# fp32 value products on two column halves of TensorE

## The chip, the cores and the metric

The kernel runs on one core of one Trainium2 chip. The metric is the device time of one execution in microseconds (us), the median over runs. Lower is better.

## The reference, cut to what matters

The program computes a causal sliding-window attention with a linear distance bias, and feeds its output to a mixture of eight experts in which every token goes to one expert.

```python
# B=8 batches, H=8 heads, S=576 positions, D=64, window 128
scores = scale * np.matmul(q, k.transpose(0, 1, 3, 2))
mask = (rel >= 0) & (rel < window)
scores = np.where(mask, scores + bias[None], -1e9)
attn = np.exp(scores - np.max(scores, axis=-1, keepdims=True))
attn = attn / (np.sum(attn, axis=-1, keepdims=True) + 1e-09)
attn_out = np.matmul(attn, v)                       # the value products
x = attn_out.transpose(0, 2, 1, 3).reshape(4608, 512)
expert_idx = np.argmax(normalized(x) @ normalized(expert_emb).T / tau, axis=1)
out[mask_e] = gate_w[mask_e, None] * (np.maximum(x[mask_e] @ w1[e], 0) @ w2[e])
```

## The kernel before

**Tiles.** The 4608 tokens are cut into 36 tiles of 128 queries: per two batches, a "first" tile and three "full" tiles of each batch, and one "pair" tile that holds the last 64 queries of both. So there are 8 first, 24 full and 4 pair tiles. Every tile is worked on in two half steps of four heads (`hf`), which makes 72 half steps.

**A half step.** `score_pe` makes the scores (a bias product on line 600 or 591, then q by k on line 613) in PSUM; it already works in 64-row and 64-column parts of the array. VectorE merges the two parts of the window (`merge_dve`) and takes the row maximum (`max_dve`, line 630). ScalarE takes the exponential (line 637). TensorE transposes the probabilities (`probs_pe`, line 645, output `ptp`), ScalarE copies them to SBUF as `pq` (line 655). GpSimd masks them into `md`, the part that meets the tile's own keys, and `mp`, the part that meets the keys of the tile before (line 664; for a pair tile `md` is the buffer `tails`, line 673). A first tile has one part alone and uses `pq` itself.

**The values.** `values_pe` (lines 685 to 706) then multiplies by the values. For each head the masked probabilities (128 keys by 128 queries, fp32) are the stationary operand and the values (128 keys by 65 columns; the last column is a constant and gives the row sum) are the moving operand. The result, queries on the partitions, goes to one PSUM bank `av`. A product of two bf16 constants (`erow`, `eone`, line 692) opens the accumulation of the sums' column. A full tile makes two products of 128 columns for each head; a pair tile makes one product of 128 columns and two of 64 columns, because its two halves have different earlier tiles; a first tile makes one. After that VectorE takes reciprocals (line 722) and normalizes (line 728), and the token rows are split in fp16 parts, transposed by a DMA (`xT`, line 759), routed, and scattered to DRAM (`xs`, line 870).

**The order.** All of attention is one static plan: class `Plan` schedules jobs with written costs (in ns), due times and buffer counts, and emits each engine's instructions in the order that comes out. The cost of the value products is on line 1085; `SWITCH` is 60 and `STEP`, the planned distance of two half steps, 2600. Every engine then runs its list in order. Near the end of attention the plan also fetches and splits the weights of the commonest expert (lines 915 to 922) and runs its first products (`ps_head`, lines 950 and 974) as filling work. After the last tile come the last routing steps, the scatters, and the experts (lines 1463 to 1652), a second plan.

Of the kernel before, what the change touches and what calls it, by code (L numbers as in the profile page):

```python
# [23 lines left out]
P = 128  # L24
# [54 lines left out]
SWITCH = 60  # L79
# [5 lines left out]
def share(T, f):  # L85
    return int((T + 1) * f + 1e-6) > int(T * f + 1e-6)
# [122 lines left out]
def kernel(  # L209
# [11 lines left out]
    nc = tc.nc  # L221
    B, _, H2, S = kx.shape
    H, D = 2 * H2, P // 2
    NTOK, DM = out.shape
    E, _, F = moe_w1.shape
# [3 lines left out]
    REM = S - NF * P  # L229
# [33 lines left out]
    def bank(what, shape, name):  # L263
        return banks["pool"].tile(shape, F32, tag=RING[what], name=name, bufs=BANKS[RING[what]])
# [17 lines left out]
    erow = const.tile([P, P], BF16, name="erow")  # L282
    eone = const.tile([P, 4], BF16, name="eone")
    nc.vector.memset(eone, 1.0)
    nc.gpsimd.memset(erow, 0.0)
    for n in (2, 1, 0):
        nc.gpsimd.affine_select(
            erow, erow, pattern=[[0, P]], compare_op=ALU.is_gt, fill=eparts[n], base=-n, channel_multiplier=1
# [170 lines left out]
    def attention(actx):  # L459
# [10 lines left out]
        qT, kT, vS = {}, {}, {}  # L470
# [81 lines left out]
        def k_blocks(T):  # L552
            kind, b, t = tiles[T]
            return [b, b + 1] if kind == "pair" else [b]
# [17 lines left out]
        def prevs(T):  # L572
            kind, b, t = tiles[T]
            if kind == "first":
                return None
            if kind == "full":
                return T - 1
            return (T - 1 - NF, T - 1)
# [39 lines left out]
        def merge_dve(T, hf, j):  # L618
            kind, b, t = tiles[T]
            ps = sc[T, hf, j]  # L620
            if kind == "full":
                m = mk["full"].unsqueeze(1).to_broadcast([P, 2, P])
                nc.vector.copy_predicated(ps[:, :, 0:P], m, ps[:, :, P : 2 * P])  # L623
            elif kind == "pair":
                m = mk["pair"][:, 0:REM].unsqueeze(1).to_broadcast([P, 2, REM])
                nc.vector.copy_predicated(ps[:, :, 0:REM], m, ps[:, :, P : P + REM])

        def max_dve(T, hf, j):
            nm_t[T, hf, j] = sm.tile([P, 2], F32, tag="nm", name=f"nm{j}_{T}_{hf}", bufs=8)
            nc.vector.tensor_reduce(nm_t[T, hf, j], sc[T, hf, j][:, :, 0:P], axis=AX.X, op=ALU.min)  # L630
# [10 lines left out]
        def probs_pe(T, hf):  # L641
            pe = pr_t.pop((T, hf))
            pt = bank("ptp", [P, 4, P], name=f"ptp_{T}_{hf}")
            for i in range(4):
                nc.tensor.transpose(pt[:, i, :], pe[:, i, :], ident)  # L645
            pq_t[T, hf] = pt
# [38 lines left out]
        def values_pe(T, hf):  # L685
            kind, b, t = tiles[T]
            md, mp = msk.pop((T, hf))
            px = bank("av", [P, 512], name=f"av_{T}_{hf}")[:, 0 : 4 * (D + 1)]
            px = px.rearrange("p (h d) -> p h d", h=4)
            xps[T, hf] = px  # L690
            pv_ = prevs(T)
            nc.tensor.matmul(px[:, :, D], erow, eone, start=True, stop=False, skip_group_check=True)
            jobs = []
            for i in range(4):
                h = 4 * hf + i
                jobs.append((0, i, 0, 0, px[:, i], md[:, i], vS[T][:, h]))
                if kind == "pair":
                    for a in range(2):
                        o = slice(a * REM, (a + 1) * REM)
                        jobs.append((1, i, 1, a, px[o, i], mp[:, i, o], vS[pv_[a]][:, h]))  # L700
                elif pv_ is not None:
                    jobs.append((0, i, 1, 0, px[:, i], mp[:, i], vS[pv_][:, h]))
            jobs.sort(key=lambda z: z[:4])
            last = max(z[2] for z in jobs)
            for _, _, n, _, o_, a_, b_ in jobs:
                nc.tensor.matmul(o_, a_, b_, start=False, stop=(n == last), skip_group_check=True)  # L706

        groups = GROUPS
# [286 lines left out]
        def then(what, u, tail=""):  # L995
            return [(f"{what}{u}{tail}", ORDER)] if u >= 0 else []

        def due(stage, u):
            return STEP * u + 1000 * DUE[stage]
# [15 lines left out]
        last = None  # L1015
        for i, (e, ns, f) in enumerate(expert_ops()):
            last, prev = f"expert{i}", last
            key = ("expert", 0)
            J(
                last, e, ns, f, after=[prev] if prev else [], due=100 * i, early=EXPERT,  # L1020
# [4 lines left out]
        for T in range(NT):  # L1025
            kind, b, t = tiles[T]
            u0 = 2 * T
            pair = kind == "pair"
# [15 lines left out]
            for hf in range(2):  # L1044
                u = u0 + hf
                a = (T, hf)
                first = kind == "first"
                dep = [f"hi_q{T}"] + k_loads + (["tab_pair"] if pair else []) + ([] if first else ["factors"])
                J(
                    f"score{u}", "PE", (960 if first else 980 if pair else 970) + SWITCH, lambda a=a: score_pe(*a),  # L1050
                    makes=[(RING["sc"], ("sc", u, j)) for j in range(2)], after=dep + then("flip", u - 2),
                    uses=[("ldq", T)] + [("k", x) for x in k_blocks(T)],
                    due=due("score", u),
                )
                for j in range(2):
                    c, key, n = a + (j,), ("sc", u, j), f"{u}_{j}"
                    J(
                        f"merge{n}", "DVE", 0 if first else 215 if pair else 328, lambda c=c: merge_dve(*c),
                        after=[f"score{u}"], uses=[key], due=due("merge", u) + 670 * j,
                    )  # L1060
                    J(
                        f"max{n}", "DVE", 330, lambda c=c: max_dve(*c), after=[f"merge{n}"], makes=[("nm", ("nm", n))],
                        uses=[key, ("nm", n)], due=due("max", u) + 670 * j,
                    )
                    J(
                        f"exp{n}", "ACT", 502, lambda c=c: exp_act(*c),
                        after=[f"max{n}"] + ([(f"exp{u}_0", ORDER)] if j else []),
                        makes=[] if j else [("pe", ("pe", u))], uses=[key, ("nm", n), ("pe", u)],
                        due=due("exp", u) + 670 * j,
                    )  # L1070
                J(
                    f"flip{u}", "PE", 452 + SWITCH // 2, lambda a=a: probs_pe(*a), after=[f"exp{u}_0", (f"exp{u}_1", -230)],
                    makes=[(RING["ptp"], ("ptp", u))], uses=[("pe", u)], due=due("flip", u),
                )
                J(
                    f"phi{u}", "DVE" if share(u, SHARE["p" if T < LATE else "p2"]) else "ACT", 592, lambda a=a: probs_act(*a), after=[f"flip{u}"], makes=[("pq", ("pq", u))],
                    uses=[("ptp", u)], due=due("phi", u),
                )
                J(
                    f"mask{u}", "POOL", 0 if first else 1260 if pair else 1188, lock=() if first else (480, 420, 600) if pair else (590, 590), emit=lambda a=a: mask_pool(*a), after=[f"phi{u}"] + (["tails"] if pair else []),  # L1080
                    makes=[] if first else [(f"tails{hf}" if pair else "md", ("md", u)), ("mp", ("mp", u))], uses=[("pq", u)], due=due("mask", u),
                )
                mk_ = [("pq", u)] if first else [("md", u), ("mp", u)]
                J(
                    f"av{u}", "PE", (480 if first else 1100 if pair else 920) + SWITCH // 2, lambda a=a: values_pe(*a),
                    after=[f"mask{u}", ] + then("put", T - XBUFS) + [f"load_v{x}" for x in k_tiles(T)], makes=[(RING["av"], ("av", u))],
                    uses=mk_ + [("v", y) for y in k_tiles(T)], due=due("av", u),
                )
                J(
                    f"recip{u}", "DVE", 95, lambda a=a: sums_dve(*a), after=[f"av{u}"], makes=[("rs", ("rs", u))],  # L1090
                    uses=[("av", u)], due=due("norm", u),
                )
                J(
                    f"norm{u}", "DVE", 332, lambda a=a: normalize(*a), after=[f"recip{u}"],
                    makes=[("xf", ("xf", T))] if hf == 0 else [], uses=[("av", u), ("rs", u), ("xf", T)],
                    due=due("norm", u) + 300,
                )
            u = u0 + 1
# [38 lines left out]
        for gi, G in enumerate(groups):  # L1137
            T0 = sum(groups[:gi])
            u = 2 * (T0 + G) - 1
# [3 lines left out]
            key = ("rank", gi)  # L1143
# [41 lines left out]
        u = 2 * GT - 1  # L1185
# [885 lines left out]
```

## Time and profile before

| what | value |
|---|---|
| median of 3 runs | 629.81 us (629.66 to 630.69) |
| the profiled execution's own time | 628.76 us |
| its span, first to last instruction | 627.0 us |
| granted TensorE clock, mean | 0.999 of full speed |
| TensorE (PE) busy | 608.8 us, 97% |
| weight loads (PEld) busy | 432.3 us, 69% |
| VectorE (DVE) busy | 464.0 us, 74% |
| ScalarE (ACT) busy | 355.6 us, 57% |
| GpSimd (POOL) busy | 256.8 us, 41% |

The busy time of an engine is the time in which at least one of its instructions was under way. Matmuls overlap one another, so the duration of one matmul is longer than its distance to the next, and a busy PE is not one at its peak; the distance of starts tells what a stream of matmuls costs. An fp32 product appears in the trace as two matmul instructions, each with a weight load of its own. In a shape such as 128*64 128x65, the first pair is the rows and columns of the stationary operand, the second the partitions and elements of the moving one.

### The profile page before, as it was taken

Reading aid. Unit: us, or ns where it says so; the run is one execution under the profiler, and the core shown is the slowest. Engines: PE = TensorE matmul, PEld = TensorE weight load, DVE = VectorE, ACT = ScalarE, POOL = GpSimd, SP = SyncE. Lnnn points to the kernel's source line nnn. Section 1 sums busy time; section 2 is a strip of 40 time slices with the busy share of each in tenths; the row PEclk is TensorE's granted clock in tenths of the full one; section 3 lists DMA queues with packets and bytes.
Section 4 is the critical chain, followed back from the end, with each engine's and each line's share of the span. In section 5 each row is a group of like instructions: output and inputs, shape, how many; then the busy total and the mean of one; then the engine's idle time right before and its main releaser. Section 6 shows DMA issues by size and latency. Waiting matters only on the chain.

```text
span 627.0 us, 15235 instructions
## 1 busy us (share of the span) xinstructions
PE 608.8 (97%) x5573; PEld 432.3 (69%) x5573; DVE 464.0 (74%) x1184; ACT 355.6 (57%) x822; POOL 256.8 (41%) x450
## 2 busy tenths in 40 slices
PE   6999999999999999999999999999999999999995
PEld 4788887888787788646465476475584764764885
DVE  4666577567758788742678778879999998789692
ACT  4777676767756787313445227447458375367441
POOL 7535457846855856750110501300403414103342
PEclk9999999999999999999999999999999999999999
DMA  8896787988997899549994945935929859516001
GB/s 215 186 157 136 194 181 182 233 183 172 231 197 163 253 229 220 135 154 304 184 295 79 338 121 106 331 89 134 323 64 290 229 91 331 125 46 174 31 2 68
DMA packets 163836, 112.48 MB, mean 179 GB/s; under 512 B 122533, under 2 KB 134821, under 8 KB 163760
## 3 DMA queue, kind: packets, MB, share of 16 engines
q1 hardware_dynamic: 153600, 85.24, 55.6%
q0 software_dynamic: 10160, 26.26, 15.3%
q8 instruction: 44, 0.72, 0.5%
q14 instruction: 32, 0.26, 0.2%
HBM read 72.93 MB, written 19.70 MB: 148 GB/s over the span
## 4 chain that ended last, share of the span: by engine, by line
PE 82%; DVE 6%; ACT 3%; DMA 3%; issue 2%; SPq 1%; POOL 1%; POOLq 0%; ACTq 0%; DVEq 0%
PE ps L1640 20%; PE av L706 18%; PE sc L613 7%; PE ptp L645 6%; PE ps7d L1483 5%; PE ps7c L1483 5%; PE ps7a L1483 5%; PE ps L1463 4%; PE sc L600 3%; PE ps7b L1483 3%; PE ps_t L1630 2%; PE ps_head L950 1%; ACT pe L637 1%; ACT w1h L1388 1%; DMA ldq<-q_dram 1%
## 5 line engine op out<-in xcount | busy, mean ns | idle before, releaser
L452 POOL DMA_INDIRECT out_dram<-y,ids x32 | 44.9, 1404 | 212.5 <-ACT y L1652 148.1
L637 ACT ACTIVATE pe<-sc,nm 128x128 f32<-128x128 f32 x288 | 85.3, 371 | 21.7 <-DVE nm L630 16.8
L1640 PE MATMUL ps<-w2h,hh 128*128 128x512 f16 x224 | 84.9, 379 | 1.3 <-ACT hh L1606 1.3
L1640 PE MATMUL ps<-w2h,hl 128*128 128x512 f16 x224 | 84.9, 379 | 0.4 <-DVE hl L1604 0.4
L1640 PE MATMUL ps<-w2l,hh 128*128 128x512 f16 x224 | 84.9, 379 | 0.0
L1640 PEld LDWEIGHTS <-hh 128*128 128x128 f16 x448 | 43.5, 98 | 53.3 <-ACT hh L1606 1.7
L706 PE MATMUL av<-v,mp 128*128 128x65 f32 (+1 forms) x512 | 79.8, 263 | 0.0
L1483 PEld LDWEIGHTS <-w1h 128*128 128x128 f16 x672 | 65.7, 98 | 14.8 <-issue 0.3
L706 PE MATMUL av<-v,md 128*128 128x65 f32 x384 | 75.6, 278 | 0.0
L655 ACT COPY pq<-ptp 128x512 f32<-128x512 f32 x72 | 42.1, 585 | 38.6 <-PE ptp L645 36.6
L706 PEld LDWEIGHTS av<-v,mp 128*128 128x128 f32 (+1 forms) x512 | 62.7, 178 | 0.7
L630 DVE TENSOR_REDUCE nm<-sc 128x2 f32<-128x256 f32 x144 | 56.1, 411 | 4.8 <-PE sc L613 4.6
L706 PEld LDWEIGHTS av<-v,md 128*128 128x128 f32 x384 | 58.5, 192 | 1.7 <-POOL ig L830 0.9
L613 PE MATMUL sc<-k,ldq 64*64 64x192 f32 (+1 forms) x1024 | 59.1, 325 | 0.0
L645 PE MATMUL ptp<-ident,pe 128*128 128x128 f32 x288 | 47.7, 285 | 3.5 <-ACT pe L637 3.0
L623 DVE COPY_PREDICATED sc<-mask_full,sc 128x256 f32<-128x256 int32 x96 | 37.6, 423 | 16.0 <-PE sc L613 14.4
L613 PEld LDWEIGHTS sc<-k,ldq 64*64 64x64 f32 (+1 forms) x1024 | 41.6, 143 | 9.8 <-issue 4.0
L755 POOL TENSOR_TENSOR gx<-xf,gx 128x512 f16<-128x512 f32 x36 | 42.1, 1169 | 13.5 <-DVE gx L744 11.5
L664 POOL TENSOR_SCALAR_AFFINE_SELECT md<-pq 128x512 f32<-128x512 f32 x48 | 31.7, 660 | 37.8 <-ACT pq L655 36.3
L722 DVE RECIPROCAL rs<-av 128x4 f32<-128x4 f32 x72 | 13.1, 181 | 46.0 <-PE av L706 45.8
L870 POOL DMA_INDIRECT xs<-gx,di x36 | 36.1, 1002 | 13.1 <-issue 5.0
L1652 ACT ACTIVATE y<-ps,gs 128x512 f32<-128x512 f32 x24 | 16.4, 682 | 44.0 <-PE ps L1640 42.4
(302 smaller groups left out, 1495.8 us busy)
## 6 DMA issues: line engine op xcount, KB each, us to landing
ws<-moe_w_dram SPq DMA_DIRECT2D x46, 512.0 KB, 7.5
ldq<-q_dram SPq DMA_DIRECT2D x36, 256.0 KB, 3.5
v<-v_dram SPq DMA_DIRECT2D x36, 256.0 KB, 4.5
ws_t<-moe_w_dram SPq DMA_DIRECT2D x12, 512.0 KB, 6.3
ws_t<-moe_w_dram POOLq DMA_DIRECT2D x12, 512.0 KB, 9.5
k<-k_dram SPq DMA_DIRECT2D x8, 640.0 KB, 6.3
stg<-moe_w_dram SPq DMA_DIRECT2D x16, 256.0 KB, 4.2
k<-k_dram SPq DMA_DIRECT2D x7, 512.0 KB, 5.8
```

What stands on the lines that cost most here:

```text
L452: ins = nc.gpsimd.indirect_dma_start(out[:, :], bass.IndirectOffsetOnAxis(ap=ids, axis=0), y, None, bounds_check=NTOK - 1, oob_is_err=False)
L613: nc.tensor.matmul(sc[T, hf, j][o, l, c], qT[T][rows, hp, o], x[rows, hp, c.start + at : c.stop + at], start=False, stop=True, skip_group_ ...
L623: nc.vector.copy_predicated(ps[:, :, 0:P], m, ps[:, :, P : 2 * P])
L630: nc.vector.tensor_reduce(nm_t[T, hf, j], sc[T, hf, j][:, :, 0:P], axis=AX.X, op=ALU.min)
L637: nc.scalar.activation(pr_t[T, hf][:, 2 * l + j, :], ps[:, l, 0:P], AF.Exp, bias=nm[:, l : l + 1], scale=-1.0)
L645: nc.tensor.transpose(pt[:, i, :], pe[:, i, :], ident)
L655: nc.scalar.copy(pq, pt)
L706: nc.tensor.matmul(o_, a_, b_, start=False, stop=(n == last), skip_group_check=True)
L755: nc.gpsimd.tensor_tensor(xx[:, DM : 2 * DM], xf_t[T], xx[:, 0:DM], op=ALU.subtract)
L870: ins = nc.gpsimd.indirect_dma_start(xs_rows[:, :], bass.IndirectOffsetOnAxis(ap=z["di"][:, g : g + 1], axis=0), X, None)
L1483: nc.tensor.matmul(ps, a[:, idx, c, fs], b[:, c, :], start=(n in OPENS and m == 0), stop=(m == len(jobs) - 1), skip_group_check=True)
L1640: nc.tensor.matmul(ps, x[:, ft, a * P : (a + 1) * P], w[:, ft, c], start=(n == 0), stop=(n == len(jobs) - 1))
```

## The change

The value products, and the product with the sums' constant, are issued for the two column halves of 64 queries each, in turn. Every product of 128 columns becomes two of 64 that write partitions 0 to 63 and 64 to 127 of the same bank; a pair tile's products with the earlier tiles had this form before. The order in a half step is now all `md` products, head by head, and then all `mp` products. The costs on the plan's line go from 480 + 30 (first), 920 + 30 (full) and 1100 + 30 (pair) to 560 + 60 and 1030 + 60.

```diff
             pv_ = prevs(T)
-            nc.tensor.matmul(px[:, :, D], erow, eone, start=True, stop=False, skip_group_check=True)
+            halves = [slice(0, 64), slice(64, P)]
+            for o in halves:
+                nc.tensor.matmul(px[o, :, D], erow[:, o], eone, start=True, stop=False, skip_group_check=True)
             jobs = []
             for i in range(4):
                 h = 4 * hf + i
-                jobs.append((0, i, 0, 0, px[:, i], md[:, i], vS[T][:, h]))
-                if kind == "pair":
-                    for a in range(2):
-                        o = slice(a * REM, (a + 1) * REM)
-                        jobs.append((1, i, 1, a, px[o, i], mp[:, i, o], vS[pv_[a]][:, h]))
-                elif pv_ is not None:
-                    jobs.append((0, i, 1, 0, px[:, i], mp[:, i], vS[pv_][:, h]))
-            jobs.sort(key=lambda z: z[:4])
-            last = max(z[2] for z in jobs)
-            for _, _, n, _, o_, a_, b_ in jobs:
+                for a, o in enumerate(halves):
+                    jobs.append((0, i, px[o, i], md[:, i, o], vS[T][:, h]))
+                    if pv_ is not None:
+                        old = pv_[a] if kind == "pair" else pv_
+                        jobs.append((1, i, px[o, i], mp[:, i, o], vS[old][:, h]))
+            jobs.sort(key=lambda z: z[:2])
+            last = max(z[0] for z in jobs)
+            for n, _, o_, a_, b_ in jobs:
                 nc.tensor.matmul(o_, a_, b_, start=False, stop=(n == last), skip_group_check=True)
...
-                    f"av{u}", "PE", (480 if first else 1100 if pair else 920) + SWITCH // 2, lambda a=a: values_pe(*a),
+                    f"av{u}", "PE", (560 if first else 1030) + SWITCH, lambda a=a: values_pe(*a),
```

## Rows read from the trace of the kernel before

**Rows 1.** Page: the chain that ended last, share of the span by engine and line.
```profile
PE 82%; DVE 6%; ACT 3%; DMA 3%; issue 2%; SPq 1%; POOL 1%; POOLq 0%; ACTq 0%; DVEq 0%
PE ps L1640 20%; PE av L706 18%; PE sc L613 7%; PE ptp L645 6%; PE ps7d L1483 5%; PE ps7c L1483 5%; PE ps7a L1483 5%; PE ps L1463 4%; PE sc L600 3%; PE ps7b L1483 3%; PE ps_t L1630 2%; PE ps_head L950 1%; ACT pe L637 1%; ACT w1h L1388 1%; D
```
**Rows 2.** Stages: us, each engine's busy us (instructions), clock, DMA share, GB/s.
```profile
15.00:75.00 60.00, 59.76 (x762) 49.92 (x762) 36.95 (x119) 42.15 (x123) 29.31 (x55) 1.00 0.78 164
...
195.00:256.00 61.00, 58.78 (x735) 48.97 (x735) 49.62 (x170) 43.34 (x121) 42.97 (x78) 1.00 0.91 209
256.00:300.00 44.00, 41.17 (x283) 24.35 (x280) 21.64 (x86) 14.28 (x32) 16.93 (x36) 1.00 0.76 218
```
**Rows 3.** Waits from 15 to 256 us: us in total, times, longest.
```profile
DVE rs L722 <- PE av L706: 45.8, 62, 1.8
ACT pq L655 <- PE ptp L645: 36.6, 49, 2.4
```
**Rows 4.** PE by line and shape: count, busy us, mean ns, idle before.
```profile
L706 PE MATMUL av<-v,md 128*128 128x65 f32 x384 | 75.6, 278 | 0.0
L706 PE MATMUL av<-v,mp 128*128 128x65 f32 x384 | 74.3, 275 | 0.0
...
L706 PE MATMUL av<-v,pq 128*128 128x65 f32 x128 | 17.3, 281 | 0.0
...
L706 PE MATMUL av<-v,tails 128*128 128x65 f32 x64 | 8.7, 278 | 0.0
...
L706 PE MATMUL av<-v,mp 128*64 128x65 f32 x128 | 5.5, 227 | 0.0
```
**Rows 5.** PE in order of time, a full tile's half step: start us, us.
```profile
57.94 0.18 PE L692 MATMUL av<-eone,erow 128*128 128x4 bf16 x1
57.98 0.41 PE L706 MATMUL av<-v,md 128*128 128x65 f32 x2
...
59.79 0.60 PE L645 MATMUL ptp<-ident,pe 128*128 128x128 f32 x4
```
**Rows 6.** The same, a pair tile's half step and a first tile's.
```profile
68.19 0.18 PE L692 MATMUL av<-eone,erow 128*128 128x4 bf16 x1
68.23 1.08 PE L706 MATMUL av<-v,tails 128*128 128x65 f32 x8
69.24 0.69 PE L706 MATMUL av<-v,mp 128*64 128x65 f32 x16
69.86 0.66 PE L645 MATMUL ptp<-ident,pe 128*128 128x128 f32 x4
...
74.87 0.18 PE L692 MATMUL av<-eone,erow 128*128 128x4 bf16 x1
74.91 1.08 PE L706 MATMUL av<-v,pq 128*128 128x65 f32 x8
75.83 0.61 PE L645 MATMUL ptp<-ident,pe 128*128 128x128 f32 x4
```
**Rows 7.** Weight loads in order of time, the pair tile's half step.
```profile
68.19 0.98 PEld L706 LDWEIGHTS av<-v,tails 128*128 128x128 f32 x8
69.24 0.55 PEld L706 LDWEIGHTS av<-v,mp 128*64 128x64 f32 x16
```
**Rows 8.** Stretches of 20 us, columns as in Rows 2.
```profile
135.00:155.00 20.00, 20.00 (x262) 17.08 (x259) 16.76 (x66) 14.77 (x45) 11.74 (x27) 1.00 0.85 189
155.00:175.00 20.00, 19.81 (x261) 15.96 (x264) 13.61 (x42) 14.39 (x43) 16.84 (x28) 1.00 0.97 237
...
215.00:235.00 20.00, 20.00 (x251) 16.77 (x250) 17.12 (x46) 16.40 (x45) 13.47 (x21) 1.00 1.16 261
235.00:256.00 21.00, 20.27 (x247) 17.26 (x244) 17.42 (x64) 12.41 (x35) 15.43 (x26) 1.00 0.76 177
```
**Rows 9.** The chain in order of time behind attention: start us, us.
```profile
258.91 5.24 DMA xT<-gx
...
287.30 5.56 DMA ws<-moe_w_dram
```

## The prediction

> **What bounds the kernel now.** I read the chain that ended last first. It is TensorE for 82% of the span, and the value products (L706) alone are 18%, the second largest line [rows 1]. Next the stages: from 15 to 75 us TensorE is busy 59.76 of 60 us, while VectorE has 36.95, ScalarE 42.15 and GpSimd 29.31; the picture holds to the end of attention near 256 us, with VectorE rising to 49.62 of 61 [rows 2]. Then the waits: what VectorE and ScalarE wait for longest in attention is TensorE, the value products (45.8 us) and the transposed probabilities (36.6 us) [rows 3]. So the engines beside TensorE have slack, and a shorter TensorE stream pulls them along until one of them is full. Last the matmuls in order of time, for what one of each kind costs [rows 4 to 7].
>
> **What one block costs now.** A full tile's half step runs from L692 at 57.94 to the next work at 59.79: 1.85 us, of which 16 instructions from 57.98 take 1.81, so 0.113 each [rows 5]. A first tile: 74.87 to 75.83, 0.96 us with 8 instructions [rows 6]. A pair tile: 68.19 to 69.86, 1.67 us [rows 6]. By counts there are 48, 16 and 8 such blocks: 128 instructions on `pq` are 16 times 8, 64 on `tails` 8 times 8, and the 384 on `md` with as many on `mp` are 48 times 16 [rows 4].
>
> **What one costs after.** The pair tile's products with the earlier tiles already have the new form, two column halves in turn. Sixteen of them begin at 69.24 and the work behind begins at 69.86: 0.62 us [rows 6]. The sixteen end 0.69 after their start and one lasts 0.227 [rows 4, 6], so the last begins 0.46 after the first: 0.031 from start to start, against 0.113 for a product of 128 columns. A fp32 product of 128 queries costs 2 x 0.031 in halves where it cost 0.113. Two things lie under that. The weight loads overlap: sixteen loads of half the columns are over in 0.55 us, where eight of 128 columns need 0.98 [rows 7]; and the matmuls of the two halves start almost together. The rest of the 0.62, 0.16 from the last start to the next work, holds the change back to the whole array, where a stream of 128 columns has 0.113: about 0.05 to 0.13 more than the pace of either form. Entering costs too: the eight before start their last at 68.23 + 1.08 - 0.278 = 69.03, and the first half begins 0.21 later, 0.10 over the pace [rows 4, 6].
>
> The Trainium skill (TensorEngine Tiling, Performance Considerations, Instruction Overhead) speaks against the change: a matmul carries some 60 cycles of overhead, and one should not take the tiling factor out of a dimension that is already small; here 65 columns move in each. By that a full block would double to some 3.8 us (a rival below). The rows just named disagree: the instruction with half the columns takes 0.031, not 0.113.
>
> **The sum on TensorE.** New block = constants, exit included in the 0.62. The constants' product was 0.04 (57.94 to 57.98) [rows 5]; two halves I put at 0.07.
> - full and pair: 0.07 + 0.62 + 16 x 0.031 = 1.19 us
> - first: 0.07 + 0.62 = 0.69 us
> - saved: 48 x (1.85 - 1.19) = 31.7; 16 x (0.96 - 0.69) = 4.3; 8 x (1.67 - 1.19) = 3.8; together 39.8 us
>
> Most blocks come behind scores, which use parts of the array too, so they change mode on entering before and after the change. I estimate 20 to 30 of 72 that come behind transposes or logits and now pay the 0.10 (2 to 3 us), and some 16 that run into scores or another value block and save an exit (1.6 us). Net 39 us. Bounds: nothing in the trace is known to make it more than about 43 (at 0.027 in place of 0.031), and below there is the serial rival.
>
> What was not shown before: both halves of a full tile read the same values, where the pair tile's halves read two different tiles. I take the shown pace, because each half still reads its own moving stream.
>
> The order of accumulation (all `md`, then all `mp`) adds no instruction. It makes `mp` needed later, so the wait for GpSimd's masks can only move later. The plan's costs add 0.11 (first), 0.14 (full) and take 0.04 (pair) per block, so the written order shifts a little; I cost that at 0, +-3 us. The new written 1.09 for a full block is near my 1.19, the old 0.95 was far from 1.85, so an order made with the new costs fits the engines better, if anything. DMAs are the same in number. Buffers: the time that is left for normalizing between two value blocks is the TensorE work between them, and that does not change.
>
> **What is given back.** Attention from 15 to 254 us is some 240 us. Taking 39 out shrinks 20 us to 16.8. Every other engine must fit its work in that. In four stretches it can't without being nearly full: VectorE has 16.76 from 135 to 155, GpSimd 16.84 from 155 to 175, VectorE 17.12 from 215 to 235 and 17.42 (of 21) from 235 to 256 [rows 8]. If an engine that works in a fixed order with waits can be 93% busy (a choice, midway between 100% and the 86% of 17.12 in 20), these stretches take 18.0, 18.1, 18.4 and 18.7 us, against 16.8 (17.6 for the last): 1.2 + 1.3 + 1.6 + 1.1 = 5.2 us back. At 100% it is about 1, at 86% with other stretches joining it is some 14. I add 1 for single waits elsewhere. DMA shares of 0.8 to 0.9 [rows 2] become about 1 if packets keep their times, but one stretch reads 1.16 [rows 8], so these shares count overlapping packets and are no floor; later loads are part of what I give back.
>
> Behind attention the last tile's chain of GpSimd split, transposing DMA (5.24 us), routing and the weights' load at 287.30 [rows 9] starts when attention ends, and filling products keep TensorE busy 41.17 of 44 us [rows 2]. I cost it as a pure shift, and the experts at 0.
>
> Time: 39 - 6 = 33 us off. The profiled execution took 628.76 (span 627.0), so 595.8; the median of the runs lies 1.05 above it, so 596.5 to 597.
>
> **The rivals.**
> - **All of it arrives.** The better order hides what I give back: 39 to 43 off, 586 to 591. For it: TensorE hardly waits now. Against: rows 8. Chance 0.17.
> - **VectorE, ScalarE and GpSimd become the bound.** At 86% busy and with longer operations where GpSimd and VectorE meet, 14 to 25 us come back: 603 to 615. For it: VectorE's 49.62 of 61 us [rows 2], which would be 49.62 of 51. Against: part of the late work (weight splits) can slide. Chance 0.25.
> - **The halves run one behind the other (slower).** Place: the 32 instructions of a full block, whose halves share the values and the array's rows. Price: 2 x 0.031 each, 0.07 + 32 x 0.062 + 0.16 = 2.21 against 1.85, so 48 x 0.36 + 16 x 0.26 = 21.4 us, about 651. It decides from 0.051 us per instruction on, (1.85 - 0.23) / 32. For it: only the pair tile shows the form, with different values. Against: rows 6. The Trainium skill (TensorE: Matmul & The Clock Gate, Part 3) says that a weight load overlaps running matmuls only where its row group differs, and both halves use all rows; the trace's sixteen loads in 0.55 us [rows 7] disagree. Chance 0.03.
> - **The instruction is the price (slower).** Each half takes 0.113, whatever its columns: a full block 0.07 + 32 x 0.113 + 0.16 = 3.8, a first 2.0, a pair 2.5, so 48 x 2.0 + 16 x 1.1 + 8 x 0.8 = 120 us, about 750. Rows 6 refute it for the pair tile. Chance 0.01.
> - **The gain is idle.** Something else paces attention and the time stays within 0.2%, about what a measurement can tell. Rows 3 speak against it: the others wait for TensorE. Chance 0.02.
>
> **How the numbers follow.** The forecast (591 to 603) has 0.50, the rivals 0.17, 0.25, 0.03, 0.01 and 0.02, and 0.02 is left below 586. From 585 to 611 lie the forecast, nearly all of the first rival and two thirds of the second: some 0.83. Faster 0.94, same 0.02, slower 0.04.
>
> **What would show it.** L706 in shapes 128*64 alone, 1792 instructions (48 and 8 blocks of 32), plus 256 of the first tiles, with starts about 0.03 apart; a full block of 1.15 to 1.25 us; 144 products on L692. VectorE's busy share in the late stretches near or over 90%, the waits for `av` much shorter, and waits of TensorE for the exponentials and masks that were not there. The stretch from the last value product to the first expert's weights as long as before. The prediction is wrong if a full block takes over 1.4 us, if TensorE waits more than about 14 us in attention, or if the stretch behind attention grows.

## The result and the profile after

The changed kernel takes 600.35 us (median of 4 runs, 599.79 to 604.13) beside 630.25 us of the kernel before in the same runs: a ratio of 0.953, 95% interval 0.948 to 0.958. The profiled execution took 599.79 us, its span 598.1 us, against 628.76 and 627.0. A second time, in another group of runs, the changed kernel took 600.30 us (ratio 0.954, 0.948 to 0.959).

The stages of the changed kernel's attention (columns: us, busy us and instructions of PE, PEld, DVE, ACT, POOL, then granted clock, DMA share, GB/s), which answer to [rows 2]:

```profile
15.00:75.00 60.00, 59.67 (x1238) 45.58 (x1236) 48.09 (x155) 49.46 (x148) 35.86 (x64) 1.00 0.96 196
75.00:135.00 60.00, 58.49 (x1205) 45.32 (x1205) 49.43 (x174) 48.72 (x146) 45.12 (x94) 1.00 1.05 237
135.00:195.00 60.00, 55.75 (x1104) 42.88 (x1096) 45.63 (x157) 44.49 (x131) 46.75 (x86) 0.97 1.09 232
195.00:220.00 25.00, 22.08 (x471) 17.31 (x472) 23.96 (x75) 20.89 (x60) 19.13 (x26) 1.00 1.08 231
```

In the first stage VectorE does 48.09 us of work where it did 36.95, and ScalarE 49.46 where it did 42.15: the work of the whole is the same, in less time. TensorE is the fullest engine up to 195 us, though it idles more from 135 us on, and from 195 to 220 us VectorE is fuller (23.96 of 25).

The matmuls of the changed kernel in order of time (start us, us), a full tile's half step and a first tile's, which answer to [rows 5, 6]:

```profile
71.26 0.20 PE L694 MATMUL av<-eone,erow 128*64 128x4 bf16 x2
71.31 0.66 PE L706 MATMUL av<-v,md 128*64 128x65 f32 x16
71.81 0.63 PE L706 MATMUL av<-v,mp 128*64 128x65 f32 x16
72.37 0.41 PE L600 MATMUL sc<-brow,bcol 64*64 64x512 bf16 x4
...
63.60 0.20 PE L694 MATMUL av<-eone,erow 128*64 128x4 bf16 x2
63.65 0.66 PE L706 MATMUL av<-v,pq 128*64 128x65 f32 x16
64.24 0.41 PE L600 MATMUL sc<-brow,bcol 64*64 64x512 bf16 x4
```

A full block goes from 71.26 to 72.37, 1.11 us, where it took 1.85; a first one 0.64, where it took 0.96. A pair tile's block now equals a full one (58.04 to 59.16). Sixteen starts fill 0.50 us (71.31 to 71.81), 0.031 each.

Waits in attention of the changed kernel, 15 to 220 us (us in total, times, longest), against [rows 3]:

```profile
DVE rs L722 <- PE av L706: 15.8, 30, 1.1
ACT pq L655 <- PE ptp L645: 12.1, 19, 1.5
...
PEld ptp L645 <- ACT pe L637: 8.3, 24, 1.3
```

VectorE's wait for the value products falls from 45.8 to 15.8 us, ScalarE's for the transposes from 36.6 to 12.1. The transposes' weight loads wait 8.3 us for exponentials, where it was 3.7.

**Where the time came from.** The last value product, the last rank product and the experts' first and last products on line 1463 are four marks. Each line of the view of one source line ends its times with the first and the last start. Before:

```profile
L706 PE MATMUL av<-v,mp x512: 219/275/324, 20.9 to 255.0; 128*128 128x65 f32 x128, 128*64 128x65 f32 x43
...
L811 PE MATMUL ptr<-acc,ones x5: 170/182/189, 150.8 to 270.9; 128*128 128x64 bf16 x2, 128*128 128x48 bf16 x1, 128*128 128x32 bf16 x1, 128*128 128x16 bf16 x1
...
L1463 PE MATMUL ps<-xT,w1h x192: 286/306/313, 284.8 to 336.8; 128*128 128x288 f16 x64, 128*128 128x352 f16 x64, 128*128 128x336 f16 x64
```

After:

```profile
L706 PE MATMUL av<-v,mp x896: 219/222/315, 20.5 to 219.4; 128*64 128x65 f32 x180
...
L811 PE MATMUL ptr<-acc,ones x5: 169/183/189, 129.1 to 235.8; 128*128 128x64 bf16 x2, 128*128 128x48 bf16 x1, 128*128 128x32 bf16 x1, 128*128 128x16 bf16 x1
...
L1463 PE MATMUL ps<-xT,w1h x192: 286/306/313, 251.4 to 306.5; 128*128 128x288 f16 x64, 128*128 128x352 f16 x64, 128*128 128x336 f16 x64
```

The last value product comes 35.6 us earlier, the last rank 35.1, the first expert product 33.4, the last on line 1463 30.3, and the end 28.9 (627.0 to 598.1). By the blocks' prices 48 x (1.85 - 1.11) + 16 x (0.96 - 0.64) + 8 x (1.67 - 1.11) = 45.1 us of TensorE were saved. So about 10 us of these have not arrived at the last rank, and 6 more are lost behind it. In the second profile of the changed kernel the five marks come 33.5, 33.1, 31.3, 30.5 and 28.7 us earlier.

Not all of the 10 us are waits. From 15 us to the last value product, before and after:

```profile
15.00:255.00 240.00, 236.68 (x3004) 198.08 (x3003) 168.42 (x575) 168.78 (x485) 149.03 (x276) 1.00 0.85 191
15.00:219.40 204.40, 195.39 (x3997) 150.69 (x3995) 166.50 (x558) 163.56 (x482) 146.71 (x267) 0.99 1.04 223
```

TensorE's idle time grows from 3.3 to 9.0 us, by 5.7 (by 7.1 in the second profile). Its busy time shrinks by 41.3 us. Of these some 2.5 are not saved but moved: of the filling products on line 950, at 0.16 us each, 24 start before the last value product in the kernel before and 8 in the changed one. So the net saving on TensorE is some 39 us. The 6 us between 45 and 39 lie mostly around the blocks: up to there the transposes (line 645) are busy 48.6 us where it was 45.2, and some blocks ran at a lower clock (last section).

### The profile page after: what moved, and what is told of

It is laid out like the page before. It is cut to its first block, busy times and chain, and to the rows that moved or that the text cites. A ratio compares the mean times of both kernels' runs of the same rounds, so it can differ in the third digit from the quotient of the medians.

```text
span 598.1 us, 17296 instructions
## 1 busy us (share of the span) xinstructions
PE 572.4 (96%) x6605; PEld 387.4 (65%) x6605; DVE 465.5 (78%) x1184; ACT 352.4 (59%) x822; POOL 268.4 (45%) x450
## 4 chain that ended last, share of the span: by engine, by line
PE 73%; DVE 10%; DMA 6%; ACT 4%; POOL 3%; issue 3%; SPq 1%; ACTq 0%; POOLq 0%; DVEq 0%
PE ps L1640 24%; PE av L706 7%; PE ps7d L1483 6%; PE ps7c L1483 6%; PE ps7a L1483 6%; PE sc L613 5%; PE ptp L645 5%; PE ps L1463 5%; PE ps7b L1483 3%; DMA ldq<-q_dram 2%; ACT pe L637 2%; PE sc L600 2%; PE ps_t L1630 2%; POOL xs L870 2%; DMA out_dram<-y_head,ids_head 1%
## 5 line engine op out<-in xcount | busy, mean ns | idle before, releaser
L452 POOL DMA_INDIRECT out_dram<-y,ids x32 | 57.1, 1783 | 215.5 <-ACT y L1652 145.1
L645 PE MATMUL ptp<-ident,pe 128*128 128x128 f32 x288 | 51.1, 294 | 5.6 <-ACT pe L637 3.6
L655 ACT COPY pq<-ptp 128x512 f32<-128x512 f32 x72 | 42.5, 590 | 16.7 <-PE ptp L645 12.1
L645 PEld LDWEIGHTS ptp<-ident,pe 128*128 128x128 f32 x288 | 31.7, 143 | 17.5 <-ACT pe L637 10.6
L1640 PEld LDWEIGHTS <-hl 128*128 128x128 f16 x224 | 22.1, 98 | 28.9 <-DVE hl L1604 2.2
L1463 PE MATMUL ps<-xT,w1h 128*128 128x288 f16 (+2 forms) x192 | 39.8, 302 | 0.0
L1483 PEld LDWEIGHTS <-w1l 128*128 128x128 f16 x336 | 32.9, 98 | 6.6
L664 POOL TENSOR_SCALAR_AFFINE_SELECT mp<-pq 128x512 f32<-128x512 f32 x56 | 36.9, 658 | 0.5
```

What stands on the lines that cost most here:

```text
L452: ins = nc.gpsimd.indirect_dma_start(out[:, :], bass.IndirectOffsetOnAxis(ap=ids, axis=0), y, None, bounds_check=NTOK - 1, oob_is_err=False)
L655: nc.scalar.copy(pq, pt)
L664: nc.gpsimd.affine_select(o_, i_, pattern=[[0, 4 * P // w], [sg, w]], compare_op=op, fill=0.0, base=0, channel_multiplier=-sg)
L1463: nc.tensor.matmul(ps[:, :w], a[:, kt, fs], xx[:, b + kt, c0 : c0 + w], start=(n == 0), stop=(n == len(jobs) - 1))
L1483: nc.tensor.matmul(ps, a[:, idx, c, fs], b[:, c, :], start=(n in OPENS and m == 0), stop=(m == len(jobs) - 1), skip_group_check=True)
L1640: nc.tensor.matmul(ps, x[:, ft, a * P : (a + 1) * P], w[:, ft, c], start=(n == 0), stop=(n == len(jobs) - 1))
```

## The experiments

**One half behind the other.** The same instructions and plan, but the four heads of one half follow one another before those of the other half.

```diff
-                    jobs.append((0, i, px[o, i], md[:, i, o], vS[T][:, h]))
+                    jobs.append((0, a, px[o, i], md[:, i, o], vS[T][:, h]))
...
-                        jobs.append((1, i, px[o, i], mp[:, i, o], vS[old][:, h]))
+                        jobs.append((1, a, px[o, i], mp[:, i, o], vS[old][:, h]))
```

> The changed kernel, but the products of one column half come one behind the other (four heads of half 0, then four heads of half 1) and no longer in turn; same instructions, same plan. Theory (the gain is two column halves working at once, 0.029 us from start to start): with one half at a time only its own weight load and stream count, 0.055 to 0.06 each, so a full block goes from 1.06 to about 1.9 us, TensorE is the bound of attention again, and the time is 640 to 655 us, slower than the kernel before the change. Rival (the gain is only that a load of 64 columns is shorter and loads run ahead, in any order): the block stays within 0.1 of 1.06 us and the time at 598 to 604 us.

Measured: 614.62 us, ratio 0.974 (0.970 to 0.978). The order alone costs 14 us, so the rival falls; but the price was between the two. The matmuls in order of time of this run:

```profile
57.41 0.20 PE L694 MATMUL av<-eone,erow 128*64 128x4 bf16 x2
57.47 0.78 PE L706 MATMUL av<-v,md 128*64 128x65 f32 x13
58.02 0.27 PE L706 MATMUL av<-v,mp 128*64 128x65 f32 x1
58.08 0.22 PE L706 MATMUL av<-v,md 128*64 128x65 f32 x1
58.13 0.22 PE L706 MATMUL av<-v,mp 128*64 128x65 f32 x1
58.13 0.22 PE L706 MATMUL av<-v,md 128*64 128x65 f32 x1
...
58.92 0.36 PE L600 MATMUL sc<-brow,bcol 64*64 64x384 bf16 x4
```

The block is 1.51 us (57.41 to 58.92). In the middle, products on `mp`, which are later in the list, start between those on `md`: where the lists of the two halves meet, several products of the second half run beside the last ones of the first. Starts of one half are some 0.06 apart (on `md` 58.08 and 58.13). Three such meetings in a block are why it was dearer than 1.11 and cheaper than the 1.9 expected; the next run tests this.

**Only one meeting.** All products of half 0, then all of half 1.

```diff
-                    jobs.append((0, i, px[o, i], md[:, i, o], vS[T][:, h]))
+                    jobs.append((a, 0, i, px[o, i], md[:, i, o], vS[T][:, h]))
...
-                        jobs.append((1, i, px[o, i], mp[:, i, o], vS[old][:, h]))
+                        jobs.append((a, 1, i, px[o, i], mp[:, i, o], vS[old][:, h]))
-            jobs.sort(key=lambda z: z[:2])
+            jobs.sort(key=lambda z: z[:3])
...
```

> The changed kernel, but all products of half 0 first and then all of half 1, so that the halves meet once in a block and not three times as in the run half by half. Theory (a half alone costs 0.057 us from start to start, as that run showed between its borders, so two cost what a whole product costs, and all gain comes from starts that fall together): a full block 1.7 to 1.9 us, the time 622 to 633 us, no gain left over the kernel before. Rival (the shorter weight load has a gain of its own): a full block of 1.5 us or less, 615 us or less.

Measured: 631.23 us, ratio 1.001 (0.998 to 1.004): the whole gain is gone, as the theory had it. A block of this run:

```profile
61.02 0.20 PE L694 MATMUL av<-eone,erow 128*64 128x4 bf16 x2
61.08 0.66 PE L706 MATMUL av<-v,md 128*64 128x65 f32 x8
61.57 0.46 PE L706 MATMUL av<-v,mp 128*64 128x65 f32 x5
...
62.89 0.36 PE L600 MATMUL sc<-brow,bcol 64*64 64x384 bf16 x4
```

It takes 1.87 us (61.02 to 62.89), the 1.85 of a full block before. Eight instructions of one half take 0.49 us (61.08 to 61.57), 0.061 each, and two of those are no cheaper than one of 128 columns at 0.113. The gain is the two halves at work at once, all of it.

**The written costs, each way.** The changed kernel with the plan's old costs, and the kernel before with the new ones.

```diff
-                    f"av{u}", "PE", (560 if first else 1030) + SWITCH, lambda a=a: values_pe(*a),
+                    f"av{u}", "PE", (480 if first else 1100 if pair else 920) + SWITCH // 2, lambda a=a: values_pe(*a),
```

> The changed kernel with the plan's old written costs (510, 950 and 1130 in place of 620 and 1090): same products, another order of the work. Theory (the gain is the shorter products, the written costs only shift the order): within 5 us of the changed kernel, 597 to 605 us. Rival (the new costs are what keeps the other engines fed): 607 us or more, with more than 5 us more of TensorE waiting in attention.

> The kernel before the change with the new written costs and the old products. Theory (TensorE is full in attention whatever the order): within 3 us of the kernel before, 627 to 634 us. Rival (the order alone brings part of the gain): 625 us or less.

Measured: with the old costs 605.98 us (ratio 0.961, 0.956 to 0.965), with the new costs alone 628.90 us (0.997, 0.995 to 1.000). The old costs' 605.98 lies between what the two theories named: 5.6 us above the changed kernel's 600.35, though the ends of the two ratios' intervals overlap (0.956 and 0.958). TensorE idles 14.6 us from 15 us to the last rank product there, against 9.4. The new costs alone stay where their theory had them. The products bring most of the gain, the order made with the new costs some 5 us more once the products are short, and next to nothing (2 us at most) while they are long. That small net effect hides a larger shift: with the new costs and the old products the last value product comes 5.0 us earlier than before (250.0 against 255.0), the end only 0.4 (626.6 against 627.0).

**The constant on 128 columns.** The product with the sums' constant whole again.

```diff
-            for o in halves:
-                nc.tensor.matmul(px[o, :, D], erow[:, o], eone, start=True, stop=False, skip_group_check=True)
+            nc.tensor.matmul(px[:, :, D], erow, eone, start=True, stop=False, skip_group_check=True)
```

> The changed kernel, but the product with the sums' constant is on 128 columns again, so that TensorE changes between the whole array and column halves once more inside each of the 72 blocks. Theory (a change of mode costs about 0.1 us on TensorE, most of which shows): a block takes 0.08 to 0.15 us more, 6 to 11 us of TensorE in all, and the time rises by 4 to 9 us. Rival (attention is bound by other engines by now, so that a little more TensorE work is hidden): under 2 us more.

Measured: 597.65 us (597.35 to 599.53), ratio 0.948 (0.943 to 0.952). The theory falls: the time does not rise. The block itself is 0.08 us dearer (a first tile's 0.72, 63.98 to 64.70, against 0.64), as the theory had it. But behind transposes that is made up ahead of the constant: from the start of the four transposes to the constant it is 0.49 us (63.49 to 63.98), in the changed kernel 0.59 (63.01 to 63.60). Behind scores it is not made up: from their start to the work behind the block it is 1.48 us (64.94 to 66.42) against 1.40 (64.48 to 65.88). That other engines hide this rest, as the rival says, is not shown. It is the lowest time of the study, but against 600.35 and 600.30, measured in other groups of runs, 0.4% is not settled: the intervals of the ratios overlap.

**What the waits hang on.** Four edits each took one suspect away. Queries and keys were loaded earlier, with one more buffer (`QBUFS` 5, `DUE['load']` -18.9 in place of -13.7). GpSimd's subtraction for the tokens' low part became a memset. Logits were planned later, with a fourth buffer, and once more with the whole constant. VectorE's split of the expert weights' low part became a memset.

```diff
-KBUFS, QBUFS = 3, 4
+KBUFS, QBUFS = 3, 5
...
-            nc.gpsimd.tensor_tensor(xx[:, DM : 2 * DM], xf_t[T], xx[:, 0:DM], op=ALU.subtract)
+            nc.gpsimd.memset(xx[:, DM : 2 * DM], 0.0)
...
-after=[(f"xdma{T}", 1500 if T < NT - 3 else 0), enc_done]
+after=[(f"xdma{T}", 5500 if T < NT - 3 else 0), enc_done]
...
-            nc.vector.scalar_tensor_tensor(lo, hd["x", i], SW, hi, op0=ALU.mult, op1=ALU.subtract)
+            nc.vector.memset(lo, 0.0)
```

> The changed kernel itself, beside the runs of this call: 599 to 604 us; the whole constant's 597.65 us of the call before is then the same within 0.5%, or faster by it if this stays at 600 or more.

> The changed kernel with five query buffers in place of four, and all query and key loads due two half steps earlier in the plan. Theory (part of the gain is given back to loads that land late, as the waits for the queries' load near 89 and 194 us show): the waits of ScalarE for the query load fall from 6.1 us to under 2, and the time to 594 to 598 us. Rival (VectorE and GpSimd pace attention, the loads' waits only sit where these would wait anyway): within 2 us of the changed kernel, 598 to 603 us.

> The changed kernel with GpSimd's subtraction for the low fp16 part of the tokens (36 of 1.17 us) left out and a memset in its place, so the low part is zero; the plan and the order are the same. Theory (GpSimd's full stretches, and VectorE's operations beside them, give back part of the gain): 36 x 0.8 us less GpSimd work takes 4 to 8 us off, 592 to 596 us. Rival (the loads, or VectorE by itself, are what holds): under 2 us off, 598 us or more.

Measured in one group of runs: the changed kernel 600.30 us (ratio 0.954, 0.948 to 0.959), early queries 601.66 (0.952, 0.946 to 0.958), light GpSimd 598.74 (0.948, 0.943 to 0.952). The waits for the query loads in attention, of the changed kernel and with early loads:

```profile
ACT ldq L550 <- DMA ldq<-q_dram: 6.1, 7, 2.1
```

```profile
ACT ldq L550 <- DMA ldq<-q_dram: 2.2, 1, 2.2
```

The wait fell by 4 us and the time did not: the rival's time came, and the late query loads are not what ends last (the edit also makes another order, so this is less sharp than the other runs). With some 23 us less on GpSimd (busy 123.16 us from 15 us to the last value product, against 146.71) the time moves by 1.6 us, inside the overlap of the intervals: below the 4 to 8 us that the theory asked, so GpSimd is no bound by itself either. The profiled execution of that run was the longest of its five (604.73 us).

> The changed kernel with the logits planned 4 us later behind their transposing load (5500 ns in place of 1500 in the plan, except for the last three tiles) and four buffers for the transposed tokens in place of three; the products are unchanged. Theory (TensorE, which runs its list in order, gives time back where logits stand at its head and their load has not landed): the waits of logits of over 0.3 us, 3.7 us in the changed kernel, go to under 1 us, and the time to 595 to 598 us. Rival (what is waited for there is late for every engine, so the wait moves to the next work in line): 599 us or more.

> The run before with the sums' constant on 128 columns as well. Theory (the whole constant costs nothing, as the mode is changed anyway behind transposes and logits): within 2 us of the run before. If the 597.65 us that the whole constant gave alone was an order or a run of luck, 599 us or more.

> The changed kernel without VectorE's split of the low fp16 part of the commonest expert's weights (16 operations of 0.6 to 0.95 us, most of them in the last 25 us of attention); a memset writes zeros there, so that part is left out of the products. The plan and order are unchanged. Theory (VectorE, busy 23.96 of 25 us from 195 to 220 us, is the bound of the last stretch): the last rank product comes 3 to 8 us earlier and the time is 592 to 597 us. Rival (VectorE is full but not what ends last): under 2 us off, 598 us or more.

> The run without the low split once more, since the kernel before took 658 us instead of 630 in the call of the first. Theory (VectorE, busy 23.96 of 25 us from 195 to 220 us, bounds the last stretch of attention): against the changed kernel's profile the last value product of 219 us comes 3 to 8 us earlier, and the time is 592 to 597 us beside a kernel before of 630. Rival (something else ends last there too): 598 us or more.

In these two groups of runs the kernel before took 657.90 and 652.55 us, so only ratios can be read. Late logits: 620.94 us, 0.946 (0.939 to 0.954). With the whole constant: 620.39 us, 0.944 (0.938 to 0.951). No low split: 615.42 us, 0.938 (0.930 to 0.946), and again 613.35 us, 0.943 (0.938 to 0.948). The waits of TensorE in the run with late logits have a row that the changed kernel lacks:

```profile
PE av L706 <- issue: 7.0, 11, 1.1
```

TensorE stood still inside blocks without any engine to wait for (a row of this kind, 3.2 us in two waits, is in the run with the old costs too), so the expected times can't be tested there. The ratios point down against 0.954, most for the run without VectorE's split, but the second of that pair overlaps the changed kernel's interval. Their last value product does not come ahead of 219 us, as the theory of the second of them asked, but at 231.5 and 226.7, in groups in which the kernel before was 28 and 22 us longer as well. Whether VectorE bounds the last stretch stays open, and so does the effect of later logits.

## Why the prediction was right

The forecast was 33 us off, 596.5 us, and 29.9 were measured (630.25 to 600.35). The mechanism held, and so did the two large terms: a net saving on TensorE of 39 us came out at 38 to 39 by the two profiles, and 6 us given back in attention at 5.7 to 7.1. The first is in part luck, for the blocks saved 5 us more than put down and the work around them cost about as much more. What was missed lies behind attention. Point by point:

- **TensorE paces attention.** Shown: an order that makes the same instructions dear again gives the whole time back (631.23 us).
- **The price of a half, 0.031 us, read from the pair tile.** Right, and the halves' shared values change nothing. The serial rival's mechanism was real only where the halves are not issued in turn. There a half alone costs some 0.06 (0.061 in the run with one meeting), above the 0.051 from which that rival decides. The Trainium skill (TensorEngine Tiling, Key Properties) says that different tiles can load weights and multiply in parallel; 1.11 us in turn against 1.87 us one behind the other agrees.
- **The block.** Put at 1.19 us, measured 1.11; the first tile's 0.69 is 0.64. The constants take 0.05 us for 0.07, the last sixteen products with the exit 0.56 for 0.62. Saved 45.1 us in place of 39.8. (The upper bound of 43 for 0.027 in place of 0.031 is added up wrongly: 2048 instructions at 0.004 us less are 8.2 us, which makes 47.)
- **The entry, at 2 to 3 us less 1.6 for saved exits.** Its price of 0.10 is right (0.59 against 0.49 us behind transposes, in the run with the whole constant). But 38 blocks stand behind transposes or logits in the order as it came out, not 20 to 30, and the transposes behind value products are dearer too (four take 0.66 us, at 65.88, where it was 0.60, at 59.79): the work around the blocks took up what the blocks saved beyond the forecast.
- **The order, at 0 +- 3.** Mis-sized: with old costs the changed kernel takes 5.6 us more. The text had the sign ("fits the engines better, if anything").
- **Given back in attention, 6 us.** TensorE's idle time grew by 5.7 us, in the second profile by 7.1. The place was right in the main: it idles from 135 us on, 4.25 us in the third stage and 2.92 in the last. The reason is shown in part only: the limit of 93% was too low, for VectorE reached 96% from 195 to 220 us, and single waits of TensorE, for exponentials and transposing loads, take more than the 1 us that I gave them. One such wait, on the chain of the changed kernel in order of time:

```profile
137.47 0.96 POOL xs L870
...
139.68 1.12 POOL gx L755
140.80 0.03 POOL spare L869
140.82 6.73 DMA xT<-gx
147.55 0.05 issue
147.60 0.26 PE ptl L765 x4
...
148.08 1.47 PE av L706 x32
...
149.55 1.83 PE av L706 x32
```

Logits stood at the head of TensorE's list until 147.60 for a load of 6.73 us that began at 140.82, after GpSimd had first run a row of scatters, the last at 137.47, two masks and the split.

- **Behind attention a pure shift, at 0.** This step failed: between the last value product and the end 6.7 us are lost, 4.8 in the second profile. One of the prediction's own signs of being wrong came with it: the stretch from the last value product to the first expert product grew from 29.8 to 32.0 us. The stretch from the last rank to the first expert product and the stage of line 1463, before and after:

```profile
270.90:284.80 13.90, 13.90 (x72) 6.34 (x71) 3.81 (x25) 1.37 (x2) 6.78 (x14) 1.00 0.67 191
284.80:336.80 52.00, 50.31 (x335) 32.42 (x334) 31.75 (x55) 21.12 (x38) 6.01 (x7) 1.00 0.85 227
```

```profile
235.80:251.40 15.60, 15.60 (x80) 7.11 (x79) 3.13 (x18) 1.87 (x3) 7.75 (x16) 1.00 0.66 190
251.40:306.50 55.10, 51.86 (x335) 32.94 (x334) 33.00 (x63) 21.34 (x38) 6.19 (x7) 0.97 0.81 214
```

In the first stretch TensorE is full in both kernels, and 8 filling products more are left for it after the change (73 on lines 950 and 974 where it was 65), 0.21 us each: that is work moved out of attention and no wait. It is 15.6 us in the run with the new costs and the old products too (last rank at 265.8, first expert product at 281.4) and 14.0 in the run with the old costs and the new products (244.1 and 258.1): the written order does it, not the products. The stage of line 1463 holds the same 335 products. There TensorE idles 3.2 us for 1.7, in two waits for the hidden values' parts (lines 1604 and 1606, 1.7 and 1.6 us), and the granted clock is 0.97 on average. In the second profile this stage ran at the full clock and took 52.8 us (253.5 to 306.3), so some 2 us are not there in every execution. Whether the change makes the lower clock more frequent is not shown: the run with the new costs alone has a clock of 0.97 and 54.1 us there too, with the old products. What follows the stage took 290.2 us before and 291.6 after, and 290.3 to 292.0 in the other profiles: no difference that these can tell.

The rival of all of it arriving is out, and so is that of the other engines as the bound: TensorE's idle time in attention grew by 5.7 to 7.1 us, not by 14 to 25, and no single engine holds it in the runs that could be read.

## What to carry to other kernels

Read a new form's price from the distance of its starts in the trace, not from a product's duration, and look for a place where the kernel already uses the form. The products on two column halves paid only when they were issued in turn: the same instructions, one half behind the other, cost what the whole columns cost. When a stream that paces a hand-planned order gets shorter, let its written cost follow: with the old costs some 5 of the 30 us were lost here. And before calling the difference of two sums a wait, look at the engine's idle time: part of it can be work that was moved or that another line now pays.

## What the runs showed of the hardware that was not expected

Where the two halves' lists meet, the trace has starts of the later list between those of the earlier one: in the run half by half, starts on `mp` and `md` lie 0.00 to 0.06 us apart around the middle meeting. A block with three meetings is 0.36 us cheaper than one with a single meeting (1.51 against 1.87).

A short wait in attention was followed by a stretch at the lower of the two clocks. In the changed kernel TensorE was busy 3.25 of 5 us, with the wait of 1.75 us that ends at 147.60, and the granted clock is below 1 in that stretch and the next (1.2 GHz for part of it, 2.4 GHz otherwise):

```profile
140.00:145.00 5.00, 5.00 (x104) 3.65 (x102) 4.12 (x14) 3.59 (x11) 4.47 (x8) 1.00 0.64 142
145.00:150.00 5.00, 3.25 (x76) 2.81 (x70) 2.81 (x10) 2.98 (x11) 4.98 (x9) 0.84 1.05 214
150.00:155.00 5.00, 5.00 (x117) 4.38 (x115) 2.99 (x10) 3.12 (x10) 4.07 (x7) 0.82 1.19 225
```

The value blocks behind that wait are dearer, 1.47 and 1.83 us on the chain of waits (148.08 and 149.55) against 1.02 for another block of 32 instructions there (93.07). So such a wait cost more than its own length here. The second profile has the same: 17.73 of 20 us busy and a clock of 0.91 from 135 to 155 us.
